# A fused attention and feed-forward kernel on one core: the first part of W_in moves to the head of GpSimd's DMA queue, the masks' distance tables move up, and later tiles are handled further ahead

## The chip, the cores and the metric

The kernel runs on one core of one Trainium2 chip. The metric is the time of one execution on the device in microseconds (us), taken as the median of seven executions. The profile is one further execution, recorded by the hardware profiler.

## The reference

Four batches with eight heads of 768 positions and head size 64 go through masked attention, and the result, seen as 3072 rows of 512, goes through two matrix products with an elementwise function between them:

```
scores = q @ k.T / 8  - slope[h] * dist          # dist = |i - j|, or 96 for the 8 global columns
keep   = (j < 8) or (0 <= i - j < 96)            # all else is masked out
x      = softmax(scores) @ v                     # 3072 x 512
h      = x @ w_in                                # 512 x 2048
out    = (h - tanh(h)) @ w_out                   # 2048 x 512
```

## The kernel before

The 3072 rows are cut into 24 tiles of 128 rows; tile u is block u // 4 of batch u % 4. A tile's attention needs only its own block of k and v (the "0" half) and, from tile 4 on, the block before it (the "1" half), into which the eight global columns are copied. The exponential's bias is not added but multiplied in afterwards, as a mask `mk` that is built once from three distance tables `rmat` ("dist" 0, 1 and 2).

The steps of one tile, with the names that the text uses and their lines:

- ("ld", "k"/"q"/"v", u), L578: a DMA from GpSimd's queue that also casts to bf16. For tile 0, k and q come instead by SyncE's queue as fp32 into `kf` (L569) and are cast by VectorE (L374). v of tile 0 and v of tile 1 come by GpSimd like the others.
- ("T", "k"/"q", u), L435: four TensorE transposes for tiles 0 to 7, with a copy out of PSUM ("Te", L372 or L374). From tile 8 on it is a DMA transpose from SyncE's queue.
- ("S", u, o), L384: scores. ("E", u, o, half), L389: exponential on ScalarE. ("M", u, o), L394: VectorE multiplies by the mask.
- ("AV", u), L403 and L405: the product with v. ("R"), L412, and ("N"), L420 or L422: the row sums' reciprocals and the scaling into `x`.
- ("Xt", u), L435, and ("X", u), L372 or L374: transposes x for tiles 0 to 5, and its copy into `xT`. From tile 6 on this too is a DMA transpose.

The rows then go through the two products in groups: tiles 0 to 3 each alone, from then on two tiles a group. ("m1", g, f), L448, is a part of the product with W_in, ("th"), L681, the tanh, ("g"), L457, the difference. The second product is "m2" (L489, L470) or, for groups 6 to 12, seven block products "P" (L316). For tiles 0 to 3, m1 with f = 0, 4, 8 and 12 needs the first, second, third and fourth part of W_in, called ("in", 0) to ("in", 3) and loaded on L546; ("out", j), L551, are the parts of W_out. The smaller `warm` matmuls on zeros (L666) fill the gaps that are foreseen on TensorE before ("S", 3, 0).

No engine chooses its order while it runs. A `Planner` simulates five engines and two DMA queues with given costs, and the sequence that it makes for each engine is what is emitted. So a change of its constants or of an op's conditions can move instructions on every engine, and the number of warm matmuls with them. Each engine, and each DMA queue, works strictly in its sequence. The list `arrive` gives the order of the transfers in GpSimd's queue: each waits for the issue of the one before. `ahead(u)` says how many tiles ahead of m1's progress tile u's attention may begin; from tile 6 on (`GATE`) its loads carry a semaphore wait for the m1 part from which they may start, half a tile (`EARLIER`) before its attention.

Of the kernel before, what the change touches and what calls it, by code (L numbers as in the profile page):

```python
# [13 lines left out]
PE, ACT, DVE, POOL, SP = ENG.PE, ENG.Activation, ENG.DVE, ENG.Pool, ENG.SP  # L14


class Planner:
# [20 lines left out]
    def run(self, free, prefer):  # L38
# [3 lines left out]
        held, freed = {}, {}  # L42
        uses, until = dict(self.uses), {}
        rings = {SP: [], POOL: []}
        setup, finish = {SP: 1.0, POOL: 1.8}, {SP: 0.35, POOL: 0.5}
        at_dma = 0.0
        mode = None
        done, start = {}, {}
# [3 lines left out]
        order = []  # L52
# [46 lines left out]
        while left:  # L99
# [5 lines left out]
            for key, n in cand:  # L105
# [4 lines left out]
                for eng, us in o["engs"]:  # L110
                    t = max(t0, free[eng])
# [16 lines left out]
            _, key, t, eng, us = best  # L128
# [38 lines left out]
def kernel(  # L167
# [47 lines left out]
    pl = Planner()  # L215
# [118 lines left out]
    def build_dist(m):  # L334
        def fill(r, base, value):
            nc.gpsimd.iota(
                r, pattern=[[1, P]], base=base, channel_multiplier=-1, allow_small_or_imprecise_dtypes=True,
            )
            if base == 0:
                nc.gpsimd.affine_select(  # L340
                    r, r, pattern=[[1, P]], base=0, channel_multiplier=-1, compare_op=ALU.is_ge, fill=value,
                )
            nc.gpsimd.affine_select(
                r, r, pattern=[[-1, P]], base=L - 1 - base, channel_multiplier=1, compare_op=ALU.is_ge, fill=value,
            )

        if m == 0:
            nc.vector.tensor_copy(out=rmat[0], in_=rmat[1])
            nc.vector.tensor_scalar_min(rmat[0][0:G, :], rmat[1][0:G, :], float(L))
        else:  # L350
            fill(rmat[m], P if m == 2 else 0, BIG)
        if m == 2:
            nc.gpsimd.memset(rmat[m][0:G, :], float(L))
# [154 lines left out]

    T_LD, T_V, T_W, T_ST, T_TR = 0.86, 1.13, 2.65, 0.4, 0.97
    AHEAD, EARLIER = 4.5, 0.5  # L510
    MORE = 0.0
    LATE = 2.0

    def ahead(u):
        return AHEAD + MORE * min(max(u - 8, 0) / 6.0, 1.0)

    arrive = [("t", 0), ("t", 1), ("t", 2), ("in", 0), ("t", 3), ("in", 1), ("in", 2), ("in", 3), ("t", 4), ("t", 5), ("out", 0), ("out", 1), ("out", 2), ("t", 6), ("out", 3), ("t", 7)]
    arrive += [("t", u) for u in range(NU) if ("t", u) not in arrive]
    GATE = 6

    prog = []
    gates = {}
    acc = 0.0
# [3 lines left out]
            prog.append((acc, ("m1", g, f)))  # L527
            acc += len(us) * per / CF

    pl.op(("dist", 1), POOL, 1.1, lambda e: build_dist(1), after=[("issue", ("ld", "k", 2))], pri=-2)  # L530
    pl.op(("dist", 0), DVE, 0.3, lambda e: build_dist(0), after=[("dist", 1)], pri=-2)
    pl.op(("dist", 2), POOL, 1.1, lambda e: build_dist(2), after=[("issue", ("in", 1))], pri=-1.5)
    for m in range(3):
        for half in range(2):
            pl.op(("mk", m, half), ACT, 0.85, lambda e, m=m, half=half: build_mask(m, half),
                  after=[("dist", m), ("mk", 0, 1) if m == 1 else None],
                  pri=-2 if m == 0 else 1)
    pl.op(("ident",), POOL, 0.6, lambda e: make_identity(nc, ident), after=[("issue", ("ld", "k", 1))], pri=-3)

    prev = None  # L540
    for it in arrive:
        kind, j = it
        if kind == "in":
            key = ("in", j)
            w = DFF // WJ
            pl.op(key, POOL, 0.8, lambda e, j=j, w=w: nc.gpsimd.dma_start(out=w_in_bf[j], in_=w_in_r[:, :, j * w : (j + 1) * w]),  # L546
                  after=[prev and ("issue", prev)], dma=T_W)
            prev = key
        elif kind == "out":
            key = ("out", j)  # L550
            pl.op(key, POOL, 0.8, lambda e, j=j: nc.gpsimd.dma_start(out=w_out_bf[j], in_=w_out_r[:, j * FJ : (j + 1) * FJ, :]),  # L551
                  after=[prev and ("issue", prev)], dma=T_W)
            prev = key
        else:
            u = j
            for nm, u in ([(nm, u) for nm in "kqv"] if u > 1 else [("k", 0), ("q", 0)] if u == 0 else
                          [("k", 1), ("q", 1), ("v", 0), ("v", 1)]):
                src = {"k": k, "q": q, "v": v}[nm]
                hw = u in hw_loads
                key = ("ld", nm, u)  # L560
                if nm == "v":
                    take = [(vname(u), ("vb", u))]
                    dst = lambda u=u: bufs[vname(u)][got["vb", u]][:, :, 0:Dh]
                else:
                    take = [(nm + "b", (nm + "b", u))]
                    dst = lambda u=u, nm=nm: buf(nm + "b", (nm + "b", u)).rearrange("p (h d) -> p h d", h=H)
                if hw and nm != "v":
                    pl.op(("ldf", nm, u), SP, 0.6,
                          lambda e, u=u, nm=nm, src=src: nc.sync.dma_start(out=buf("kf", ("kf", nm, u)), in_=rows(src, u)),  # L569
                          take=[("kf", ("kf", nm, u))], dma=T_LD)  # L570
                    pl.op(key, [(DVE, 0.43), (ACT, 0.6)], None,
                          lambda e, u=u, nm=nm, dst=dst: copy(e, dst(), buf("kf", ("kf", nm, u))),
                          after=[("ldf", nm, u)], take=take, give=[("kf", nm, u)])
                else:
                    go = [kk for a, kk in prog if a <= u - ahead(u) - EARLIER] if u >= GATE else []
                    if go:
                        gates[key] = go[-1]
                    pl.op(key, POOL, 0.88, lambda e, u=u, src=src, dst=dst: nc.gpsimd.dma_start(out=dst(), in_=rows(src, u)),  # L578
                          after=[prev and ("issue", prev), go[-1] if go else None], take=take, dma=T_V if nm == "v" else T_LD,
                          pri=-1 if u < GATE else 0)  # L580
                    prev = key

    for u in range(NU):
# [4 lines left out]
        for nm in ("k", "q"):  # L588
# [3 lines left out]
            if u < NPE:  # L592
                pl.op(("T", nm, u), PE, 0.24,
                      lambda e, u=u, nm=nm: pe_T(buf("bank", ("T", nm, u)), buf(nm + "b", (nm + "b", u))),
                      after=[("ld", nm, u), ("ident",), ("issue", last) if last else None], take=[("bank", ("T", nm, u))],
# [5 lines left out]
                      after=[("T", nm, u)], take=[(nT, tT)], give=[("T", nm, u)])  # L601
            else:
                pl.op(("T", nm, u), SP, 1.25,
                      lambda e, u=u, nm=nm, nT=nT, tT=tT: nc.sync.dma_start_transpose(
                          out=bufs[nT][got[tT]], in_=buf(nm + "b", (nm + "b", u))),
                      after=[("ld", nm, u), go], take=[(nT, tT)], give=[(nm + "b", u)], dma=T_TR, lag=LATE)
        Te = (lambda nm, u: ("Te", nm, u) if u < NPE else ("T", nm, u))
        os_ = (0, 1) if i else (0,)
        for o in os_:
# [3 lines left out]
                  after=[Te("q", u), go] + ([("issue", ("S", u, 0)), ("K", w) if i >= 2 else None] if o else [Te("k", u)]),  # L613
                  take=[("bank", ("S", u, o, hh)) for hh in range(2)] + [("po" if o else "pd", ("p", u, o))],
                  give=[("qT", u)] + (kgive if i >= 2 else []), mode="half", pri=0)
        for o in os_:
            for hh in range(2):
                pl.op(("E", u, o, hh), ACT, 0.53, lambda e, u=u, o=o, hh=hh: a_E(u, o, hh),
                      after=[("S", u, o), ("issue", ("E", u, 0, 1)) if o else None, ("issue", ("E", u, o, 0)) if hh else None],
                      give=[("S", u, o, hh)])  # L620
            pl.op(("M", u, o), DVE, 0.7, lambda e, u=u, o=o: a_M(u, o),
                  after=[("E", u, o, 0), ("E", u, o, 1)] + [("mk", 2 if o else min(i, 1), half) for half in range(2)])
        if 1 <= i < NQ - 1:
# [3 lines left out]
              after=[("M", u, 0), ("M", u, 1) if i else None, ("ld", "v", u), ("V", w) if i >= 2 else None, ("vone",)],  # L627
# [16 lines left out]
        if u < NPX:  # L644
            pl.op(("Xt", u), PE, 0.24,
                  lambda e, u=u: pe_T(buf("bank", ("X", u)), buf("x", ("x", u)).rearrange("q h d -> q (h d)")),
                  after=[("N", u, 0), ("N", u, 1), ("ident",)], take=[("bank", ("X", u))], give=[("x", u)], mode="full")
# [25 lines left out]
    for g, us in enumerate(groups):  # L673
# [65 lines left out]
        for t, u in enumerate(us):  # L739
            if u == NU - 1:  # L740
                for qq in range(4):
# [4 lines left out]
                          pri=2, mode="full")  # L746
# [32 lines left out]
    def prefer(s, at):  # L779
        return (1 if share2[at[1]] + 2.5 <= share1[at[0]] else 2) if s == 1 else (2 if share2[at[1]] + 2.5 <= share1[at[0]] else 1)  # L780

    order, done = pl.run({PE: 1.6, ACT: 2.1, DVE: 0.8, POOL: 0.7, SP: 0.7}, prefer)
    tc.plan = (order, done, pl)

    with tc.manual_schedule(engines={PE, ACT, DVE, POOL, SP}):
# [50 lines left out]
```

## Time and profile before

| | |
|---|---|
| median of 7 executions | 212.03 us (211.4 to 212.63) |
| the profiled execution | 211.4 us, its span from first to last instruction 209.6 us |
| granted TensorE clock | 0.999 |
| TensorE matmul, busy | 201.5 us, 96% of the span |
| VectorE, ScalarE, GpSimd, busy | 159.7, 143.2 and 70.1 us |
| DMA by GpSimd's queue (q0) | 13.37 MB in 77024 packets, 83.8% of the span on 16 engines |
| DMA by SyncE's queue (q1) | 13.38 MB in 32768 packets, 37.3% |

The profiled execution took as long as the shortest of the seven. Busy time of TensorE includes the 36 warm matmuls that the profile holds, which compute nothing. DMA shares of the queues overlap, so that together they may pass 100%.

### The profile page before, as it was taken

How to read it: one execution, taken by the hardware profiler on the slowest of the kernel's cores; microseconds unless marked ns; L12 is line 12 of the kernel's file. 1: busy time of each engine (PE TensorE's matmuls, PEld its weight loads, DVE VectorE, ACT ScalarE, POOL GpSimd, SP SyncE). 2: the span in 40 equal slices, each digit the busy share in tenths (PEclk: the TensorE clock that was granted, in tenths of full speed). 3: DMA queues.
4: the chain of work that ended last, by engine and by line, in shares of the span. 5: the costliest groups of instructions: out<-in, count | busy, mean ns of one | idle time of the engine just before them, and what ended most of it. 6: DMA issues, size and time to landing. Idle time of an engine off the chain costs nothing.

```text
span 209.6 us, 5798 instructions
## 1 busy us (share of the span) xinstructions
PE 201.5 (96%) x2281; PEld 161.6 (77%) x2292; DVE 159.7 (76%) x344; ACT 143.2 (68%) x349; POOL 70.1 (33%) x90
## 2 busy tenths in 40 slices
PE   5988999999999999999999999999999999999994
PEld 3757999565686766667888988988988989888853
DVE  2564798989276677759889999989999989898620
ACT  2399979678489788776776857887885784435311
POOL 7998375550055315045135225315225000000000
PEclk9999999999999999999999999999999999999999
DMA  9999999999979998999999997999999913002022
GB/s 130 122 145 190 198 166 207 182 166 185 166 122 141 133 175 125 106 153 104 174 103 86 215 128 123 153 134 138 140 118 160 127 28 117 9 3 100 0 103 100
DMA packets 109820, 27.12 MB, mean 129 GB/s; under 512 B 102497, under 2 KB 106849, under 8 KB 109793
## 3 DMA queue, kind: packets, MB, share of 16 engines
q0 software_dynamic: 77024, 13.37, 83.8%
q1 hardware_dynamic: 32768, 13.38, 37.3%
q8 instruction: 18, 0.29, 0.6%
q14 instruction: 10, 0.07, 0.1%
HBM read 27.26 MB, written 6.29 MB: 160 GB/s over the span
## 4 chain that ended last, share of the span: by engine, by line
PE 78%; issue 0%; ACT 0%
PE bank L448 34%; PE bank L316 21%; PE bank L489 12%; PE bank L384 5%; PE bank L405 2%; PE bank L403 2%; PE bank L470 2%; PE bank L435 0%; ACT ot L372 0%
## 5 line engine op out<-in xcount | busy, mean ns | idle before, releaser
L448 PE MATMUL bank<-xT,w_in_bf 128*128 128x256 bf16 (+1 forms) x896 | 97.2, 257 | 1.5 <-DMA w_in_bf<-in_moe_w_in_dram 1.4
L448 PEld LDWEIGHTS <-w_in_bf 128*128 128x128 bf16 x896 | 75.6, 98 | 12.6 <-DMA w_in_bf<-in_moe_w_in_dram 1.8
L681 ACT ACTIVATE th<-bank 128x512 f32<-128x512 f32 x96 | 56.7, 610 | 32.0 <-PE bank L448 23.4
L457 DVE TENSOR_TENSOR g<-bank,th 128x512 bf16<-128x512 f32 x80 | 53.3, 683 | 11.7 <-ACT th L681 11.6
L578 POOL DMA_DIRECT2D kb<-in_k_dram x23 | 20.6, 895 | 81.5 <-PE bank L448 57.2
L389 ACT ACTIVATE pd<-bank 128x512 bf16<-128x512 f32 x48 | 26.2, 602 | 10.2 <-PE bank L384 9.9
L316 PEld LDWEIGHTS <-hb 128*128 128x128 bf16 x280 | 27.1, 98 | 3.1
L420 ACT ACTIVATE x<-bank,rden 128x64 bf16<-128x64 f32 x104 | 23.1, 319 | 4.9 <-DVE rden L412 4.9
L290 DVE TENSOR_TENSOR hb<-g 128x1024 bf16<-128x1024 bf16 x35 | 22.9, 681 | 0.1
L578 POOL DMA_DIRECT2D vb<-in_v_dram x24 | 21.5, 897 | 3.4 <-DMA w_out_bf<-in_moe_w_out_dram 2.1
L389 ACT ACTIVATE po<-bank 128x512 bf16<-128x512 f32 x40 | 22.1, 616 | 0.0
L316 PE MATMUL bank<-bsum,hb 128*128 128x256 bf16 x168 | 21.6, 273 | 0.0
L578 POOL DMA_DIRECT2D qb<-in_q_dram x23 | 20.6, 894 | 1.4 <-DMA w_out_bf<-in_moe_w_out_dram 1.2
L394 DVE TENSOR_TENSOR pd<-pd,mk 128x1024 bf16<-128x1024 bf16 x24 | 16.5, 688 | 5.9 <-ACT pd L389 5.6
L489 PE MATMUL bank<-w_out_bf,g 128*128 128x512 bf16 x73 | 18.9, 379 | 0.4
L394 DVE TENSOR_TENSOR po<-po,mk 128x1024 bf16<-128x1024 bf16 x20 | 13.8, 689 | 2.1 <-ACT po L389 1.9
L489 PE MATMUL bank<-w_out_bf,hb 128*128 128x512 bf16 x60 | 14.8, 379 | 0.2
L384 PE MATMUL bank<-qT,kT 64*128 64x128 bf16 x352 | 14.6, 221 | 0.1
L384 PEld LDWEIGHTS <-kT 64*128 64x128 bf16 x352 | 10.3, 96 | 5.6 <-issue 5.0
L316 PE MATMUL bank<-bsum,g 128*128 128x256 bf16 x112 | 14.5, 273 | 0.0
L316 PE MATMUL bank<-w_out_bf,hb 128*128 128x256 bf16 x112 | 14.5, 273 | 0.0
L403 PE MATMUL bank<-vb,pd 128*128 128x65 bf16 x192 | 14.0, 193 | 0.0
(58 smaller groups left out, 197.1 us busy)
## 6 DMA issues: line engine op xcount, KB each, us to landing
out_dram<-ot SPq DMA_DIRECT2D x7, 512.0 KB, 3.9
vb<-in_v_dram POOLq DMA_DIRECT2D x24, 128.0 KB, 6.2
kb<-in_k_dram POOLq DMA_DIRECT2D x23, 128.0 KB, 4.4
qb<-in_q_dram POOLq DMA_DIRECT2D x23, 128.0 KB, 5.3
out_dram<-ot SPq DMA_DIRECT2D x9, 256.0 KB, 4.0
w_in_bf<-in_moe_w_in_dram POOLq DMA_DIRECT2D x4, 512.0 KB, 9.3
w_out_bf<-in_moe_w_out_dram POOLq DMA_DIRECT2D x4, 512.0 KB, 10.8
xT<-x SPq DMA_TRANSPOSE x18, 5.2
```

The costliest lines, as they stand in the source:

```text
L290: eng_of(e).tensor_tensor(out=out, in0=x, in1=y, op=ALU.add if sign > 0 else ALU.subtract)
L316: nc.tensor.matmul(o, a, b, start=(f == 0), stop=(f == CH - 1))
L384: nc.tensor.matmul(t[hh][:, p * P : (p + 1) * P], kt[r, p, :], qt[r, p, :], start=True, stop=True)
L389: nc.scalar.activation(dst, t, AF.Exp, bias=0.0, scale=scale)
L394: nc.vector.tensor_tensor(out=p, in0=p, in1=mk[:, m, :, :], op=ALU.mult)
L403: nc.tensor.matmul(o, pd[:, slot(h), :], vd[:, h, 0 : Dh + 1], start=True, stop=w is None)
L420: nc.scalar.activation(x[:, h, :], t[:, h, 0:Dh], AF.Copy, bias=0.0, scale=rd[:, h, :])
L448: nc.tensor.matmul(t[:, (f - f0) * n : (f - f0 + 1) * n], w_in_bf[j][:, c, fo : fo + P], xt[:, c, 0:n], start=(c == 0), stop=(c == CD - 1),)
L457: nc.vector.tensor_tensor(out=dst, in0=t.rearrange("q (b n) -> q b n", n=n), in1=th.rearrange("q (b n) -> q b n", n=n), op=ALU.subtract,)
L489: nc.tensor.matmul(o, gblk(g, f, f + 1, t * P, t * P + P)[:, 0, :], w_out_blk(f, 0, DM), start=(f == 0), stop=(f == CF - 1),)
L578: pl.op(key, POOL, 0.88, lambda e, u=u, src=src, dst=dst: nc.gpsimd.dma_start(out=dst(), in_=rows(src, u)), after=[prev and ("issue", prev ...
L681: pl.op(("th", g, f), ACT, 0.55, lambda e, g=g, f=f: nc.scalar.activation(buf("th", ("th", g, f)), buf("bank", ("h", g, f)), AF.Tanh, bias ...
```

## The change

The order of transfers in GpSimd's queue changes at its head: ("in", 0) comes before everything but tile 0's k and q (which are SyncE's), and ("in", 1) comes before tile 3's loads. The distance table 1, from which tables 0 and 1 are made, is built as soon as v of tile 1 has been issued, and no longer after k of tile 2. `ahead(u)` grows from 4.5 tiles at tile 8 to 5.5 tiles at tile 14 and beyond. The Planner's own constants (start of the queues, set-up and end of a DMA, 1.2 us more for a part of a weight) change as well; they cost nothing on the chip but shape the order.

```diff
-        setup, finish = {SP: 1.0, POOL: 1.8}, {SP: 0.35, POOL: 0.5}
+        setup, finish = {SP: 1.1, POOL: 2.0}, {SP: 0.3, POOL: 0.5}
...
-    MORE = 0.0
+    MORE = 1.0
     LATE = 2.0
+    W_LATE = 1.2
 
     def ahead(u):
         return AHEAD + MORE * min(max(u - 8, 0) / 6.0, 1.0)
 
-    arrive = [("t", 0), ("t", 1), ("t", 2), ("in", 0), ("t", 3), ("in", 1), ("in", 2), ("in", 3), ("t", 4), ("t", 5), ("out", 0), ...
+    arrive = [("t", 0), ("in", 0), ("t", 1), ("t", 2), ("in", 1), ("t", 3), ("in", 2), ("in", 3), ("t", 4), ("t", 5), ("out", 0), ...
...
+    DIST1 = ("ld", "v", 1)
...
-    pl.op(("dist", 1), POOL, 1.1, lambda e: build_dist(1), after=[("issue", ("ld", "k", 2))], pri=-2)
+    pl.op(("dist", 1), POOL, 1.1, lambda e: build_dist(1), after=[("issue", DIST1)], pri=-2)
...
-                  after=[prev and ("issue", prev)], dma=T_W)
+                  after=[prev and ("issue", prev)], dma=T_W, lag=W_LATE)
...
-    order, done = pl.run({PE: 1.6, ACT: 2.1, DVE: 0.8, POOL: 0.7, SP: 0.7}, prefer)
+    order, done = pl.run({PE: 1.6, ACT: 2.1, DVE: 0.8, POOL: 1.25, SP: 0.75}, prefer)
```

The sequences that come out of it differ from those before as follows (warm matmuls as "w").

- GpSimd, before: k1, identity, q1, v0, v1, k2, dist 1, q2, v2, in 0, k3, q3, v3, in 1, dist 2, in 2, in 3, k4. After: in 0, k1, identity, q1, v0, v1, dist 1, k2, q2, v2, in 1, dist 2, k3, q3, v3, in 2, in 3, k4.
- TensorE, before: 10 w, T k0, 3 w, T k1, T q0, T q1, S0, S1, 7 w, T k2, 6 w, T q2, AV0, 1 w, S2, 3 w, AV1, Xt0, 5 w, m1(0,0), Xt1, AV2, T k3, T q3, m1(1,0), Xt2, 1 w, S3, m1(2,0), m1(0,4), AV3, m1(1,4), m1(2,4), m1(0,8).
- TensorE, after: 11 w, T k0, 9 w, T q0, 2 w, S0, T k1, 2 w, T q1, 3 w, S1, 7 w, AV0, T k2, AV1, T q2, 2 w, Xt0, 4 w, S2, m1(0,0), Xt1, 5 w, AV2, T k3, m1(1,0), T q3, Xt2, m1(0,4), m1(2,0), S3, m1(1,4), m1(2,4), m1(0,8), AV3.
- VectorE after, from its sixth step: T k0's copy, cast of q0, T q0's copy, dist 0, copies of T k1 and T q1, M0, M1, both R and both N of tile 0, both R and one N of tile 1, X0, M2, X1. Before, dist 0 stood behind the copies of T q0 and T q1, tile 0's R came ahead of M1, and tile 0's N was ScalarE's.
- ScalarE after: both halves of mask 0, E0 twice, E1 twice, both halves of mask 1, copies of T k2 and T q2, N of tile 1's second half, E2 twice. Before: E0, both halves of mask 0, E0, E1 twice, half of mask 1, N of tile 0 twice, E2 twice, N of tile 1.
- SyncE after: T k9 and T q9 come ahead of the stores of tiles 1 and 2 and of X7; before, they came behind them.
- From tile 8 on, loads, transposes, S and AV of a tile stand up to one tile earlier among the m1 parts. The m1, m2 and P parts are the same in number and size.

More of the change, by code (lines that the diff above doesn't have):

```diff
@@ L510 @@
     AHEAD, EARLIER = 4.5, 0.5
-    MORE = 0.0
+    MORE = 1.0
     LATE = 2.0
+    W_LATE = 1.2
     def ahead(u):
         return AHEAD + MORE * min(max(u - 8, 0) / 6.0, 1.0)
-    arrive = [("t", 0), ("t", 1), ("t", 2), ("in", 0), ("t", 3), ("in", 1), ("in", 2), ("in", 3), ("t", 4), ("t", 5), ("out", 0), ("out", 1), ("out", 2), ("t", 6), ("out", 3), ("t", 7)]
+    arrive = [("t", 0), ("in", 0), ("t", 1), ("t", 2), ("in", 1), ("t", 3), ("in", 2), ("in", 3), ("t", 4), ("t", 5), ("out", 0), ("out", 1), ("out", 2), ("t", 6), ("out", 3), ("t", 7)]
     arrive += [("t", u) for u in range(NU) if ("t", u) not in arrive]
     GATE = 6
+    DIST1 = ("ld", "v", 1)
     prog = []
@@ L551 @@
             pl.op(key, POOL, 0.8, lambda e, j=j: nc.gpsimd.dma_start(out=w_out_bf[j], in_=w_out_r[:, j * FJ : (j + 1) * FJ, :]),
-                  after=[prev and ("issue", prev)], dma=T_W)
+                  after=[prev and ("issue", prev)], dma=T_W, lag=W_LATE)
             prev = key
```

## The prediction

> **What bounds the kernel.** I read the page's groups first, then TensorE's waits, then its busy time by stretch. In the first fence a row ends with the idle time ahead of the group and what ended it; the second is the whole list of TensorE's waits by the view of waits; the third gives stretch, its length, busy time (instructions), granted clock, DMA share and GB/s.
>
> ```profile
> L448 PE MATMUL bank<-xT,w_in_bf 128*128 128x256 bf16 (+1 forms) x896 | 97.2, 257 | 1.5 <-DMA w_in_bf<-in_moe_w_in_dram 1.4
> ```
>
> ```profile
> PE bank L435 <- DVE kb L374: 1.5, 1, 1.5
> PE bank L448 <- DMA w_in_bf<-in_moe_w_in_dram: 1.4, 2, 1.0
> PE bank L666 <- DVE zeros L668: 1.1, 1, 1.1
> PE bank L435 <- ACT x L420: 0.4, 2, 0.2
> ```
>
> ```profile
> 13.50:16.30 2.80, 1.43 (x15) 1.00 1.78 175
> 22.50:30.00 7.50, 7.50 (x142) 1.00 1.99 174
> 44.00:100.00 56.00, 55.58 (x580) 1.00 1.44 141
> 100.00:200.00 100.00, 99.95 (x1131) 1.00 1.03 108
> ```
>
> TensorE bounds the kernel from 22.5 us to the end: no wait is left and it is busy throughout. Its useful work is the same after the change, so the end moves by what the change takes from, or adds to, its idle and warm time before 22.5 us, unless it makes a new wait later. That early time is held by two arrivals of W_in, in the timeline (start, length, engine, line; in brackets the idle time before):
>
> ```profile
> 4.91 0.61 PE L435 MATMUL bank<-ident,kb 128*128 128x128 bf16 x4 [1.53 <-DVE kb L374]
> 5.90 0.71 DVE L374 CAST qb<-kf 128x512 bf16<-128x512 f32 x1
> 6.66 1.05 PE L435 MATMUL bank<-ident,qb 128*128 128x128 bf16 x8
> 7.30 0.87 DVE L374 COPY qT<-bank 128x512 bf16<-128x512 bf16 x2 [0.26 <-PE bank L435]
> 8.09 0.24 DVE L348 COPY rmat<-rmat 128x128 f32<-128x128 f32 x1
> 8.36 0.21 DVE L349 TENSOR_SCALAR rmat<-rmat 8x128 f32<-8x128 f32 x1
> 8.89 1.69 ACT L358 ACTIVATE mk<-rmat 128x128 bf16<-128x128 f32 x8
> 10.49 1.55 ACT L389 ACTIVATE pd<-bank 128x512 bf16<-128x512 f32 x3
> 16.33 1.07 PE L448 MATMUL bank<-xT,w_in_bf 128*128 128x128 bf16 x16 [1.03 <-DMA w_in_bf<-in_moe_w_in_dram]
> 21.42 1.07 PE L448 MATMUL bank<-xT,w_in_bf 128*128 128x128 bf16 x16 [0.32 <-DMA w_in_bf<-in_moe_w_in_dram]
> ```
>
> m1(0,0) starts at 16.33 with W_in's first part, m1(0,4) at 21.42 with its second. The copy of tile 0's xT ends at 14.78 + 0.42 = 15.20, so the first part is 1.1 us late.
>
> **W_in's first part first.** It removes both waits: issued at about 1.25 instead of 9.16, part 1 is in long before 15 us; part 2 is now ahead of tile 3's three loads (3 x 0.88 = 2.6 us of queue), so it lands by 21.4 - 2.6 = 18.8 us and is wanted at about 19.8, behind AV2 and m1(1,0). What is late next is tile 0's own chain, which I follow in the new sequences:
>
> - T k0 stays at 4.91. Its four loads of weights take 0.34, and nine warm matmuls stand between it and T q0. The first ten took 2.32 us from first start to last end, the last alone 0.42, so 0.21 apart: 9 x 0.21 = 1.9. T q0 starts at 7.15 (6.66 before).
> - T q0 to its copy 0.64 (6.66 to 7.30), the copy 0.42: 8.2. Dist 0 is now behind this copy and takes 0.48 (8.09 to 8.57): 8.7. GpSimd makes dist 1 by 7.4 in either order, as two moved issues balance, so it does not decide.
> - Mask 0 at 8.8, followed by the next step 1.60 later (8.89 to 10.49). E0 and E1 are four of 0.48 apart, the last 0.6: 8.8 + 1.6 + 3 x 0.48 + 0.6 = 12.4.
> - Two branches. VectorE: M1 0.68, R 0.30, both N 0.76, then R and N of tile 1 some 0.65, X0 0.42: 15.3. ScalarE: two halves of mask 1 in 1.6, the copies of T k2 and T q2 0.5 and 0.6: 15.1, then S2 with 0.34 on TensorE. m1(0,0) starts at about 15.5, 0.8 earlier than before.
> - Part of that is given back. AV2 needs M2: N of tile 1 0.9, two E 1.1, M 0.68, and three hand-overs of 0.1, from 15.1: 17.9. TensorE fills the time with Xt1 and five warm matmuls.
>
> From AV2 on I see no wait. Before m1(1,4), AV2, T k3, T q3, Xt2, S3, m1(1,0), m1(2,0) and m1(0,4) are issued; AV3, which stood ahead of it, now comes later. In issue time: 0.27 + 3 x 0.24 + 0.34 + 3 x 0.89 = 4.0, so m1(1,4) starts at 21.9; with the 0.27 of AV3 still owed, that compares as 22.2 with 22.57 before. The gain is 0.4 us. Bounds: 0.8 (all of m1(0,0)'s gain is kept) and, if k1 and q1 land so late that S1 holds E1, about zero.
>
> The last case needs a price: in 0 now stands ahead of every GpSimd load. During W_in alone the DMA moves at this rate:
>
> ```profile
> 20.00:22.00 2.00, 0.71 (x2) 1.00 1.24 206
> ```
>
> 0.524 MB at 206 GB/s are 2.5 us. k1, issued at 1.25, landed 4.4 later, at 5.65; it then lands at about 8.2, q1 at 9.0, v0 at 9.9, v1 at 10.8, q2 at 12.5. AV0 wants v0 at 12.1 and T q2 its load at 13. q1 must be in by 9.6 for S1 to reach E1 in time. That is hidden by 0.6 us, and this cover is thin: when it is gone, each us of q1's delay costs as much at the end.
>
> **The masks' distances.** Dist 1 goes ahead of k2's issue: k2 is 1.1 us later in GpSimd's sequence, which the transfer of in 0 hides, since the DMA is behind the issues by then. Cost nothing; without the cover, T k2 has another 0.8 us before the copy on ScalarE wants it.
>
> **Later tiles further ahead.** Loads and attention of tiles after 8 come up to a tile earlier. Loads wait in GpSimd's queue for an m1 part or a free buffer; GpSimd has 50 us and more of idle time and nobody waits for its next instruction. SyncE's queue now has T k9 and T q9 ahead of X7; X7 landed at 58.6 where m1 wanted it at 62.2, 3.6 us of cover against two issues of 1.3. TensorE has no wait after 22.5 us that could go, so the profiled execution gains nothing here; I take zero. Its bounds: -0.6 (the seven runs spread from 211.4 to 212.63 and the profiled one is at the lower end, so others may hold such a wait) and +0.6 (as much, made anew).
>
> **The sum.** The profiled execution took 211.4 us, 1.8 more than its span: 211.4 - 0.4 = 211.0. The median lies 0.63 above that execution; I keep the distance: 212.03 - 0.4 = 211.6.
>
> **Rivals.** (a) *Tile 0's q is held up by in 0.* The fp32 loads of tile 0 are on SyncE's queue, and now meet a weight part on the same engines instead of a small load:
>
> ```profile
> kf<-in_k_dram SPq DMA_DIRECT2D x1, 256.0 KB, 3.3
> kf<-in_q_dram SPq DMA_DIRECT2D x1, 256.0 KB, 4.0
> ```
>
> q0 landed at 1.27 + 4.0 = 5.3 and was cast at 5.90. k1, on the other queue, landed at 5.65, so that the two overlapped at their ends. If what is left of q0 must wait for all of in 0, it lands at 7.8, T q0 starts at 8.55 and not 7.15, and everything in the list above is 1.4 later: 1.4 - 0.4 = 1.0 slower, 213.0. It decides from the point where T q0 starts after 7.55 (no gain left), that is q0 after 6.8. For it speaks that dist 0 and so mask 0 now hang behind T q0's copy; against it, that q0 landed 1.2 us after tile 0's k although k1 was coming in: 0.262 MB in 1.2 us are 218 GB/s, no slower than W_in alone.
>
> The Trainium skill ("DMA: Bandwidth & Descriptors", Queues, rings and completion order) says that a DMA engine changes between queues only after a whole packet of some 9 to 17 descriptors. By that rule alone q0's rest would wait for large packets of the weight, once or twice, and the sum would go towards this rival's 213.0, and by the row of q0 beside k1 it stays at 211.6; no run here shows the two together.
>
> (b) *More is gained.* Part 2 of W_in, which TensorE waited for at 21.42, comes with 1 us or more to spare; executions longer than the profiled one may have waited longer for it. Then the whole spread above the fastest goes too: 212.03 - 0.4 - 0.6 = 211.0. For it: both early waits are for transfers. Against: no trace shows a longer run.
>
> (c) *A new wait in the steady part*, such as X behind T in SyncE's queue: 0.5 to 1 us, 212.3. Against it is the cover of 3.6 us above.
>
> **How the numbers follow.** Forecast 0.43, (a) 0.28, (b) 0.21, (c) 0.08. A measurement of this kernel tells about 0.3%, 0.64 us, from no change. The forecast, from 210.9 to 212.1 in its own bounds, is mostly inside that and a quarter of it faster; (b) is faster; of (a) three quarters are slower, of (c) half. Faster 0.33, same 0.41, slower 0.26. The range reaches from (b)'s 210.9 to just past (a), 213.1.
>
> **What would show it.** Right: T q0 at about 7.2, m1(0,0) at 15.5 and no wait for w_in_bf in TensorE's waits; nothing new after 23 us. Wrong: a cast of qb after 6.8 (rival a), an S1 that waits for q1's load, TensorE waits for kT or qT after 44 us (c), or more than 0.8 us gained (b).

## The result, and the profile after

The median of the kernel after is 213.71 us (27 executions) against 212.02 for the kernel before (64 executions beside it); the ratio is 1.0052 (95% interval 1.0034 to 1.007). The ratio leaves out executions more than 1.5% above the fastest of their kernel, seven of the 27 here, which the medians hold: the loss is 1.1 us by the ratio and 1.7 us by the medians. The forecast was 211.6 us, 0.4 us faster. The profiled execution took 213.74 us, its span is 211.9 us, 2.3 us more than before.

TensorE's waits (line, what it waited for, us in total, times, longest) have lost W_in, as forecast, and got others:

```profile
PE bank L435 <- DVE qb L374: 2.0, 1, 2.0
PE bank L435 <- DVE kb L374: 1.2, 1, 1.2
PE bank L668 <- DVE zeros L670: 1.1, 1, 1.1
PE bank L384 <- DMA qT<-qb: 0.9, 1, 0.9
PE bank L403 <- DVE pd L394: 0.8, 2, 0.4
```

The 1.4 us for `w_in_bf` are gone; 2.0 us for tile 0's cast q are new, and so are 0.9 us of a scores step for a transposed q. The stretches (length, TensorE's busy time, weight loads, VectorE, ScalarE, GpSimd, granted clock, DMA share, GB/s) show that the second lies late, where the kernel before had 99.95 of 100 us:

```profile
22.50:30.00 7.50, 7.50 (x142) 7.29 (x140) 5.54 (x13) 6.56 (x18) 4.48 (x6) 1.00 2.05 172
100.00:200.00 100.00, 99.11 (x1102) 86.95 (x1100) 88.77 (x175) 63.93 (x148) 20.14 (x23) 1.00 0.97 101
```

The timeline of the kernel after, at the lines shown of before:

```profile
8.54 0.65 DVE L374 CAST qb<-kf 128x512 bf16<-128x512 f32 x1 [2.71 <-DMA kf<-in_q_dram]
9.24 0.61 PE L435 MATMUL bank<-ident,qb 128*128 128x128 bf16 x4 [1.96 <-DVE qb L374]
11.73 0.63 PE L435 MATMUL bank<-ident,qb 128*128 128x128 bf16 x4
17.59 1.07 PE L448 MATMUL bank<-xT,w_in_bf 128*128 128x128 bf16 x16
21.61 1.95 PE L448 MATMUL bank<-xT,w_in_bf 128*128 128x128 bf16 x32
111.34 0.62 PE L384 MATMUL bank<-qT,kT 64*128 64x128 bf16 x16 [0.89 <-DMA qT<-qb]
```

T q0 runs at 9.24 (forecast 7.15), T q1 at 11.73, m1(0,0) at 17.59 (forecast 15.5, before 16.33); m1(0,4) does not wait for W_in any more, and S of tile 16 waits at 111.34. Two of the signs of being wrong that the prediction named are here: a cast of qb after 6.8 (8.54) and a wait for qT after 44 us. Three rows of the DMA issues (queue, KB, us from issue to landing) say what came late at the start:

```profile
w_in_bf<-in_moe_w_in_dram POOLq DMA_DIRECT2D x1, 512.0 KB, 8.2
kf<-in_q_dram SPq DMA_DIRECT2D x1, 256.0 KB, 7.2
kb<-in_k_dram POOLq DMA_DIRECT2D x1, 128.0 KB, 8.2
```

W_in's first part, issued at 1.25, took 8.2 us. Tile 0's q took 7.2 (4.0 before), and tile 1's k, issued at 2.14, landed at 10.29 (5.65 before, forecast 8.2); tile 1's q followed at 11.13 (forecast 9.0, wanted by 9.6).

A ledger helps with all that follows. m1(0,8), the product with W_in's third part, is the first step after which TensorE is full but for the waits named below, and the last block of m2 (the second half of L470) is one of the last. Both starts are from the trace (us); the sum is the start of the last block. Waits that the text gives to the hundredth are how far a step starts behind its place, 0.03 to 0.14 us more than the idle time in the views.

| kernel | m1(0,0) | m1(0,8) | from there to the last block | sum |
|---|---|---|---|---|
| before | 16.33 | 24.36 | 181.25 | 205.61 |
| after | 17.59 | 25.62 | 182.28 | 207.90 |
| e8, after once more | 17.73 | 25.56 | 182.19 | 207.75 |
| e1, k1 first | 15.51 | 24.08 | 182.82 | 206.90 |
| e9, half a part first | 15.43 | 24.04 | 182.30 | 206.34 |
| e7, k1 first and slack | 15.97 | 23.99 | 181.75 | 205.74 |
| e12, part first and slack | 16.43 | 24.46 | 181.74 | 206.20 |
| e10, k1 and q1 first, slack | 17.10 | 25.48 | 181.75 | 207.23 |
| e4, before with `MORE = 1.0` | 16.27 | 25.30 | 181.66 | 206.96 |
| e11, before with slack | 15.97 | 24.26 | 182.08 | 206.34 |

The loss of 2.29 us between these two executions is 1.26 before m1(0,8) and 1.03 after it. In the new sequence AV3 (0.25 us, from 22.32 to 22.57 in the kernel before) stands behind m1(0,8) and no longer ahead of it, so the loss is about 1.5 early and 0.75 late.

### The profile page after: what moved, and what is told of

Same layout as the page of the kernel before. It is cut to its first block, busy times and chain, and to the rows that moved or that the text cites. A ratio compares the mean times of both kernels' runs of the same rounds, so it can differ in the third digit from the quotient of the medians.

```text
span 211.9 us, 5815 instructions
## 1 busy us (share of the span) xinstructions
PE 201.9 (95%) x2291; PEld 162.4 (77%) x2301; DVE 160.9 (76%) x347; ACT 141.4 (67%) x340; POOL 70.1 (33%) x90
## 4 chain that ended last, share of the span: by engine, by line
PE 76%; DMA 11%; ACT 5%; issue 4%; DVE 1%; POOL 1%; SPq 0%; POOLq 0%; ACTq 0%
PE bank L448 34%; PE bank L316 18%; PE bank L489 12%; PE bank L384 5%; DMA kf<-in_q_dram 3%; DMA qb<-in_q_dram 3%; DMA qT<-qb 2%; PE bank L403 2%; DMA kT<-kb 2%; PE bank L405 2%; PE bank L435 2%; PE bank L470 2%; ACT mk L358 2%; ACT pd L389 1%; ACT x L420 1%
## 5 line engine op out<-in xcount | busy, mean ns | idle before, releaser
L457 DVE TENSOR_TENSOR g<-bank,th 128x512 bf16<-128x512 f32 x80 | 53.4, 683 | 10.3 <-ACT th L683 10.1
L420 ACT ACTIVATE x<-bank,rden 128x64 bf16<-128x64 f32 x96 | 21.2, 314 | 3.0 <-DVE rden L412 3.0
L384 PEld LDWEIGHTS <-kT 64*128 64x128 bf16 x352 | 10.3, 95 | 6.8 <-issue 5.5
## 6 DMA issues: line engine op xcount, KB each, us to landing
w_out_bf<-in_moe_w_out_dram POOLq DMA_DIRECT2D x4, 512.0 KB, 11.4
```

The lines of the kernel that those rows point to most:

```text
L384: nc.tensor.matmul(t[hh][:, p * P : (p + 1) * P], kt[r, p, :], qt[r, p, :], start=True, stop=True)
L420: nc.scalar.activation(x[:, h, :], t[:, h, 0:Dh], AF.Copy, bias=0.0, scale=rd[:, h, :])
L457: nc.vector.tensor_tensor(out=dst, in0=t.rearrange("q (b n) -> q b n", n=n), in1=th.rearrange("q (b n) -> q b n", n=n), op=ALU.subtract,)
```

## The experiments

Theory 1: in 0 holds up tile 0's q (rival (a)). Theory 2: it holds up tile 1's k and q behind it in GpSimd's queue, beyond the cover of 0.6 us. Theory 3: the new places of the later tiles make waits of their own.

**e1: tile 1's k first.** The order of two issues on GpSimd is exchanged; every other sequence is as in the kernel after.

```diff
+    swap = [("in", 0), ("ld", "k", 1)]
+    at = [next(i for i, o in enumerate(order) if o[2] == kk) for kk in swap]
+    a, b = order[at[0]], order[at[1]]
+    order[at[0]], order[at[1]] = (b[0], b[1], *a[2:]), (a[0], a[1], *b[2:])
```

> The changed kernel with every engine's sequence kept, except that GpSimd issues k of tile 1 first and W_in's first part second. Theory 1 (W_in's first part, coming first on the shared DMA engines, holds back the rest of tile 0's fp32 q, and mask 0, E0 and all behind hang on that q): with a small load between them q0 lands at 5.3 to 5.6 instead of 8.5, T q0 starts at 7.2, m1(0,0) at 15.6 instead of 17.6, m1(1,4) at 22.0 instead of 23.8; 1.7 us less, 212.0 us, ratio to before 1.000. Theory 2 (it is tile 1's loads behind W_in that come too late for S1): q1, v0 and v1 stay where they are, T q0 stays at 9.2, at most 0.3 us less, ratio 1.006. Theory 3 (the loss is made by the later tiles' new places): nothing moves, ratio 1.008.

Measured: 212.98 us, ratio 1.0028 (0.9995 to 1.0062). The timeline has T q0 at 7.08 and m1(0,0) at 15.51, which the prediction had as 7.15 and 15.5:

```profile
7.08 0.55 PE L435 MATMUL bank<-ident,qb 128*128 128x128 bf16 x4
10.17 0.40 PE L435 MATMUL bank<-ident,qb 128*128 128x128 bf16 x4 [1.07 <-DMA qb<-in_q_dram]
15.51 1.07 PE L448 MATMUL bank<-xT,w_in_bf 128*128 128x128 bf16 x16
```

So the prediction's chain through tile 0 holds here, though T q1 still waits for q1. The time of 212.0 us that theory 1 expected is missed: m1(0,8) comes 1.5 us earlier, but the end only 1.0, since S of tile 16 now waits 1.06 us and S of tile 18 0.34. It does not tell theory 1 from 2, as q0 too landed in time.

**e2, e3, e4: the parts of the change alone.** e2 is the kernel after with `MORE = 0.0` (no growth of the lead), e3 the kernel before with the new `arrive` and the earlier dist 1 and all its own constants, e4 the kernel before with `MORE = 1.0`.

> The changed kernel with later tiles as far ahead as before (MORE = 0.0). Theory 1: the first 45 us are unchanged, q0 lands late at about 8.5 and m1(0,0) starts at about 17.6; only the wait of 1.0 us ahead of S of tile 16 may go: 212.7 to 213.7 us, ratio 1.003 to 1.008. Theory 3 (the later tiles' places are the whole loss): 212.0, ratio 1.000.

> The kernel before with GpSimd's new order alone (W_in's first part first, its second ahead of tile 3, distance 1 behind the second v); the planner's constants and the later tiles as before. Theory 1: q0 lands at about 8.5 here too, but in this sequence distance 0 and mask 0 stand ahead of q0's cast, so less hangs on it: T q0 at about 9.3, m1(0,0) at 16.5 to 16.8, total 212.3 to 213.5 us, ratio 1.001 to 1.007. Theory 3: as the kernel before, 1.000. Were q0 not late, T q0 would still wait for T k1 ahead of it, at about 9.0, so its landing and not T q0 tells.

> The kernel before with later tiles up to one tile further ahead alone (MORE = 1.0). Theory 1: the early part is as before (m1(0,0) at 16.3), no new wait that matters, 212.0 within 0.4 us, ratio 0.998 to 1.002. Theory 3: most of the loss shows here, 213 to 213.7 us, ratio 1.005 to 1.008.

| | time, us | ratio | what TensorE waits for |
|---|---|---|---|
| e2 | 217.36 | 1.0218 (1.0158 to 1.0278) | 2.3 us for qT at tile 20 |
| e3 | 213.76 | 1.0066 (1.0035 to 1.0097) | 2.1 us for k1, 0.6 us for qT at tile 22 |
| e4 | 213.48 | 1.0053 (1.0019 to 1.0087) | m1(0,4) 1.3 us for W_in's second part |

No part gains by itself. e2 missed both expectations (212.7 to 213.7, and 212.0): from m1(0,8) on its profiled execution took 186.05 us, and with the wait of 2.3 us at tile 20 came a granted clock of 0.50 from 150.7 to 154.1 us; the rest of its loss was not followed up. e3 shows the head's loss without any replanned lead: q0 landed 3.8 us after its issue, in time, and k1 8.1 after its own:

```profile
PE bank L435 <- DMA kb<-in_k_dram: 2.1, 1, 2.1
```

e4 has no wait for a transposed q, and e2, with a shorter lead, has the largest, so it is not the longer lead alone that makes these waits; the change's other constants move the loads and transposes as well. Still e4 has the time that theory 3 expected (213.0 to 213.7) and theory 1 did not (212.0 within 0.4). In its profiled execution 0.94 us are lost up to m1(0,8) and 0.41 from there on, without a wait. The first is at a place where the kernel before waits as well: W_in's second part let m1(0,4) start at 22.37 in this execution and at 21.42 in that of before. All DMA issues up to W_in's last part, at 15.0 us, stand within 0.03 us of those of before, and no transfer of SyncE's queue runs between 5.3 and 47.9 us, so nothing in this trace leads from the longer lead to that landing. Why the twelve executions of e4 are slower remains open.

**e8: the kernel after, unaltered, on another chip.**

> The changed kernel again, unaltered, for a second profile and on one chip with the next three. Theory 1 in the form that the first runs leave (q0's rest meets W_in's first part on single DMA engines, so the delay differs from run to run: q0 landed 7.2, 6.3 and 3.8 us after its issue in three kernels with this head of the queue): q0 lands anywhere from 5 to 9 us, 213.5 us, ratio to before 1.005, and the runs spread wider than those of before. Were the delay a fixed cost of the order, it would be 8.5 again within 0.3.

Measured: 212.9 us, ratio 1.0034 (1.0013 to 1.0055). This execution separates theories 1 and 2 by itself, because q0 happened to land in time:

```profile
7.09 0.63 PE L435 MATMUL bank<-ident,qb 128*128 128x128 bf16 x4
10.52 0.61 PE L435 MATMUL bank<-ident,kb 128*128 128x128 bf16 x4 [1.66 <-DMA kb<-in_k_dram]
```

T q0 is at 7.09, yet T k1 waits 1.66 us for a k1 that landed at 10.47, and m1(0,0) starts at 17.73, no earlier than the 17.59 with q0 late. Theory 1 falls as the cause: the loss is as large with q0 in time. In the profiled execution of the kernel after, q0's delay comes on top of k1's by at most the 0.6 us that T k1 (10.90) started behind k1's landing (10.29).

**e5: e1 with the later loads released half a tile earlier.**

```diff
-                        gates[key] = go[-1]
+                        gates[key] = [kk for a, kk in prog if a <= u - ahead(u) - EARLIER - 0.5][-1]
```

> e1 (k of tile 1 ahead of W_in's first part, all sequences of the changed kernel otherwise) with the later tiles' loads allowed half a tile (some 3.7 us) earlier by their semaphore waits; sequences kept. Theory 4 (what is left of the loss is S waiting for the transposed q, since the load of q, its transpose and the neighbours' transfers come close to each other in the new places): loads land earlier, the waits for qT (1.3 us in e1, at tiles 16 and 18) go, 1.0 to 1.4 us less than e1: 211.6 to 212.0, ratio 0.998 to 1.000. Rival (the DMA engines as such are the limit there, earlier loads only take from the transposes before them): as e1, ratio 1.003, with waits at other tiles.

Measured: 213.08 us, ratio 1.004 (1.0011 to 1.0069). The waits moved to S of tiles 17 (0.38 us), 18 (0.55) and 21 (0.52), and T q4 waited 0.87. The rival's numbers came: earlier loads alone do not heal the late term. That the DMA engines are the limit there, which is the rival's reason, was not shown.

**e6 and e7: e1 replanned with slack.** The Planner allows 1 us more for each DMA transpose, a longer lead from the start and loads a whole tile ahead; `MORE` is 0.5 in e6, 0 in e7.

```diff
-    AHEAD, EARLIER = 4.5, 0.5
-    LATE = 2.0
+    AHEAD, EARLIER = 5.0, 1.0
+    LATE = 3.0
```

> e1 with the later tiles planned anew: a DMA transpose reckoned 1 us longer (LATE = 3.0), loads a whole tile ahead of the attention (EARLIER = 1.0), attention 5.0 to 5.5 tiles ahead (AHEAD = 5.0, MORE = 0.5). Theory 4: no wait for qT, the early gain of 0.1 to 0.4 us is kept: 211.6 to 212.0, ratio 0.998 to 1.000, and runs spread less. Rival: the loss is in the more frequent changes between score and full matmuls (38 after 44 us, 36 in e1): no better than e1, 1.003.

> As e6 with MORE = 0.0 (attention 5.0 tiles ahead throughout). Theory 4: as e6 or 0.2 us more (40 changes of matmul kind after 44 us): 211.8 to 212.2, ratio 0.999 to 1.001; so that slack and not MORE decides. Rival (being further ahead is what costs): better than e6 by 0.5 us or more.

Measured: 211.86 us, ratio 1.0006 (0.9983 to 1.0028), and 211.99, ratio 0.9996 (0.9977 to 1.0016). No wait for a transposed q is left in either; it lands 2.7 us or more ahead of its scores (e1: 0.14 us and less at tiles 11, 16 and 18). With both causes removed the kernel is as fast as before, and not faster.

**e9: half of W_in's first part first.** The kernel after, with the part cut into two DMAs: the first half stands where the part stood, the second (`w_in_rest`) behind tile 1's q.

```diff
+            nc.gpsimd.dma_start(out=w_in_bf[0][:, :, 0 : w // 2], in_=w_in_r[:, :, 0 : w // 2])
...
+    q1 = pl.ops[("ld", "q", 1)]["fn"]
+    pl.ops[("ld", "q", 1)]["fn"] = lambda e: (q1(e), w_in_rest())
```

> The kernel after with all sequences kept, but W_in's first part goes in two halves: its first half at the head of GpSimd's queue, its second half (of the same 0.26 MB) behind tile 1's q. Theory (tile 1's k and q wait for the bytes ahead of them): k1 landed at 6.2 with nothing ahead of it and at 10.3 to 10.5 with the whole part ahead, so with half of it at about 8.3, q1 at 9.1, T q1 at 9.2 to 9.5, and m1(0,0) at 15.5 to 15.9 instead of 17.6; the late wait of the 16th tile's scores stays, ratio to before 1.002 to 1.004. Rival (the first weight transfer is late by itself, whatever its size): k1 at 9.5 or later, m1(0,0) at 17 or later, ratio 1.005.

Measured: 212.2 us, ratio 1.0014 (0.9991 to 1.0038). k1 landed at 7.66, q1 at 8.71, T q1 ran at 9.16, m1(0,0) at 15.43, a little better than expected. So it is bytes ahead of k1 that cost, not that a weight comes first: k1 lands at 5.93 to 6.83 with no weight ahead (e1, e5, e6, e7, e14, e16), at 7.66 with 0.26 MB, at 9.70 to 10.47 with 0.52 MB (after, e2, e3, e8, e12, and e13 and e15 below). The late term is still there (182.30 us after m1(0,8)), but at another place: S of tile 16 got its q 0.26 us ahead, and T q4 waited for its load, 0.94 us behind its place. Less these waits, the kernel after (0.93), e1 (1.06 and 0.34) and e9 all take 181.35 to 181.42 us after m1(0,8). With the 0.25 of AV3 the kernel before would have 181.5, so these waits are as large as the late term.

**e10: k1 and q1 both ahead of W_in's first part, with e7's slack.**

> The replanned kernel with more slack (a transpose given 1 us more, loads a whole tile ahead, no growth of the lead), sequences kept, with tile 1's k, the identity and tile 1's q all ahead of W_in's first part. It had 211.99 us with T q1 at 10.63 and m1(0,0) at 15.97. Theory (m1(0,0) hangs on tile 1's q as long as q lands after 9.6, then on the masks): q1 lands at about 7, T q1 runs at 8.5 to 9.2, m1(0,0) at 15.1 to 15.5, no late wait; 211.3 us, ratio 0.995 to 0.998. Rival (the masks' chain on VectorE and ScalarE already sets m1(0,0)): m1(0,0) within 0.2 of 15.97 and 212.0, ratio 1.000. The price to watch is the first part of W_in, wanted at 15.1: it should land at about 10.

Measured: 213.19 us, ratio 1.0053 (1.0027 to 1.0079); both expectations failed. T q1 ran at 8.98, as hoped, but what stands behind the part is now v0, and AV0 waited for it:

```profile
PE bank L435 <- DMA kb<-in_k_dram: 1.3, 1, 1.3
PE bank L403 <- DMA vb<-in_v_dram: 1.2, 1, 1.2
```

The first row is T k2. After these two waits TensorE's clock was halved, as the stretches show (columns as above):

```profile
14.00:15.50 1.50, 1.24 (x21) 1.10 (x22) 0.64 (x3) 0.75 (x2) 1.50 (x3) 1.00 1.43 201
16.00:19.00 3.00, 3.00 (x29) 2.39 (x28) 0.92 (x2) 2.55 (x11) 2.15 (x3) 0.50 2.15 171
19.50:21.00 1.50, 1.50 (x31) 1.48 (x30) 1.26 (x6) 1.41 (x4) 1.01 (x2) 1.00 1.35 200
```

m1(0,8) starts at 25.48; from there it takes e7's 181.75 us to the hundredth. Nine of the twelve executions had a mean granted clock of 0.992 or less; the other three took 211.57, 211.85 and 213.8 us.

**e11: the kernel before with the slack alone.**

> The kernel before with the slack alone: a transpose given 1 us more, a lead of 5 tiles, loads a whole tile ahead; head of GpSimd's queue as before. Theory (the slack only heals waits that the new places made; the kernel before has none): m1(0,0) at 16.3, m1(0,4) at about 21.4, no late wait, 212.0 us, ratio 0.998 to 1.002. Rival (the slack is worth something of its own, and the two kernels with it hide a loss that the queue's head makes): 211.0 or less, ratio under 0.997.

Measured: 212.89 us, ratio 1.0051 (1.0022 to 1.008). Neither: the slack costs. TensorE waits nowhere late, but from m1(0,8) on it takes 182.08 us against 181.25. In the new sequence it changes 42 times between scores and other matmuls after 45 us, against 36 before and in the kernel after; e7 has 40. A step of 16 score matmuls takes 0.55 us from its first matmul to the next product, and two steps of 8 take 0.66, so that scores cost more when they stand apart. How much more is easily read wrongly: the traces of the kernel after, e7 and e11 lack 10 or 11 of the 144 m2 matmuls, and a score step seems 0.23 us longer where the record behind it is missing. So the same program has 12.16 us of scores from m1(0,8) on in e7 and 11.48 in e16, whose records are complete, and the kernel after 11.72 in its first profile and 11.27 in e13; the kernel before has 11.27, with no step lengthened. The slack thus costs some 0.2 us of scores in e7 and e16, and in e11 (12.30, less two lengthened steps 11.85) up to 0.6 of its 0.8; the rest of e11's loss is open. The 12.2 us against 11.3 in the expectation of e16 below do not compare like with like.

**e12: the slack with W_in's part first.**

> The kernel after with the slack (a transpose given 1 us more, loads a whole tile ahead, no growth of the lead), W_in's first part at the head of GpSimd's queue as in the change. Against the same kernel with tile 1's k first (211.99) only the first two transfers differ. Theory (the queue's head costs at the end what it costs at m1(0,0) as soon as no late wait is left): k1 lands at 10.3, m1(0,0) at 17.4 to 17.9, no late wait; 1.3 to 1.9 slower, 213.3 to 213.9 us, ratio 1.006 to 1.009. Rival (the early loss is made up later, and the late waits alone make the change slower): 212.0 to 212.6, ratio under 1.003.

Measured: 212.54 us, ratio 1.0025 (1.0004 to 1.0046): the rival's numbers, but not its reason. k1 landed at 9.70, earlier than in the two profiles of the kernel after, and m1(0,0) started at 16.43, 0.46 later than in e7. The end is 0.46 later too (206.20 and 205.74): the early term is smaller here than expected, but it goes to the end undiminished where no late wait is met.

These 0.46 us are not q1's landing, which is 10.54 here and 10.58 in e7. They arise behind it (T q1 and S1, first of e7, then of e12):

```profile
10.63 0.40 PE L435 MATMUL bank<-ident,qb 128*128 128x128 bf16 x4 [0.82 <-DMA qb<-in_q_dram]
11.54 0.40 PE L384 MATMUL bank<-qT,kT 64*128 64x128 bf16 x8 [0.19 <-DVE qT L374]
10.58 0.62 PE L435 MATMUL bank<-ident,qb 128*128 128x128 bf16 x4
11.78 0.61 PE L384 MATMUL bank<-qT,kT 64*128 64x128 bf16 x8
```

The same matmuls take half as long again in e12. In every trace TensorE begins at half of its later pace: warm matmuls start 0.213 us apart, later 0.109. The full pace comes at 7.4 us in e1, 10.0 in e7, 11.1 in the kernel before, 13.2 in e12, 13.9 in the kernel after and 16.5 in e8. The views print a clock of 1.00 for this time, since the trace's record of the granted clock begins only with the full pace. With k1 first, five of six executions run at the full pace from 10.0 us on (e14 falls back from 11.8 to 15.2); all seven with the part first run at half pace between 12.2 and 13.1, three of them because they fell back (e3, e13, e15). So the part ahead of k1 costs in two ways: q1, which is behind both in either order, lands somewhat later (median 10.86 against 10.55), and tile 1's transposes and scores run more slowly. With the part first TensorE stands idle before T k1 (0.9 us in e12, 1.66 in e8); that this idling is what keeps the pace low was not tested.

**e13 to e16: two by two on one chip.** The kernel after had 213.71 us in the first measurement and 212.9 on another chip (e8), a difference as large as the terms, so the four combinations were run side by side: W_in's part or k1 first, the change's sequences or those with slack. e13 is the kernel after, e14 as e1, e15 as e12, e16 as e7.

> The unaltered kernel after, beside the next three on one chip, as a table of two by two: W_in's first part or tile 1's k at the head of GpSimd's queue, with the sequences of the change or those with slack. Theory (two terms that add: the head's loss early, 0.5 to 1.5 us at the third quarter of W_in, m1(0,8), and the later tiles' places 0.5 to 1 us from there to the end): 213.3 to 213.8 us, ratio 1.005 to 1.008, m1(0,8) at 25.5 and 182.2 us from there to the last matmul of m2. Rival A (the later places make all of it): the same here. Rival B (the head makes all of it): the same here.

> The kernel after with tile 1's k ahead of W_in's first part, sequences kept: the early term is taken away, the late one stays. Two terms: 0.5 to 1.2 us less than the unaltered kernel after, 212.4 to 212.9 us, ratio 1.002 to 1.004; m1(0,8) at 24.1, 182.3 to 182.8 from there. Rival A (the later places make all of it): as the unaltered kernel after within 0.3 us. Rival B (the head makes all of it): as the kernel before, ratio within 0.0015 of 1.

> The slack's sequences with W_in's first part at the head as in the change: the late wait is taken away, the early term stays. Two terms: 0.4 to 1.0 us less than the unaltered kernel after, 212.4 to 213.0, ratio 1.002 to 1.005; m1(0,8) at 24.5 to 25.5 and 181.75 from there. Rival A: as the kernel before, ratio within 0.0015 of 1. Rival B: as the unaltered kernel after.

> Both taken away: the slack's sequences and tile 1's k first. Two terms: 211.9 to 212.1, ratio 0.999 to 1.001; m1(0,8) at 24.0 and 181.75 from there. That nothing is gained is put down to score matmuls standing apart: 40 changes between scores and other matmuls after 44 us in TensorE's sequence against 36 in the kernel before, and 12.2 us for the scores after m1(0,8) against 11.3.

| | the change's sequences | with slack |
|---|---|---|
| W_in's part first | 213.58, ratio 1.0079 (1.0048 to 1.011) | 212.69, 1.0014 (0.9985 to 1.0042) |
| k1 first | 212.71, 1.0035 (1.0018 to 1.0053) | 211.68, 1.0002 (0.9981 to 1.0022) |

By the medians, exchanging the first two transfers takes away 0.87 us, the slack 0.89, both 1.90; by the ratios it is 0.9, 1.4 and 1.6 us. The executions of one cell spread over 1.3 to 2.2 us, and e13 has only six, so that the two terms add is shown to no better than about 1 us. Rival A (the later places make all of it) fails at e14, 0.87 us below e13 where it asked for 0.3 at most, though e15's ratio is as near to 1 as it asked. Rival B (the head makes all of it) fails at e14's ratio and at e15's time. The late term is plain in the traces: from m1(0,8) on e13 took 182.38 us and e14 181.87, e15 and e16 181.75 each. The early term is not: m1(0,8) is at 24.44, 25.27, 24.59 and 24.08 in e13 to e16, where 25.5 was expected of e13 and 24.1 of e14. In e14's profiled execution W_in's part landed only at 10.29 and T q1 waited 2.0 us for q1, although k1 came first; in e13's it landed at 8.94. The clock was 0.50 for 3.4 us from about 12 us on in both, and in e15's.

## Why the prediction was wrong, point by point

- **TensorE is the bound from 22.5 us, and only idle and warm time can move the end**: right for the late part, where the waits account for the late term of the kernel after, e1 and e9 within 0.15 us. For the early part the prediction left out TensorE's pace, which made 0.5 us between e7 and e12.
- **W_in's waits go**: right; neither part of it is waited for.
- **Tile 0's chain gives m1(0,0) at 15.5**: right as a chain (15.51 in e1, 15.43 in e9), but it had the case where nothing ahead of it is late.
- **"From AV2 on I see no wait", and the gain of 0.4**: wrong. Where m1(0,0) did start at 15.5, TensorE waited for tile 3's loads, which the change puts behind W_in's second part: T q3 in e1 and T k3 in e9.

```profile
19.61 0.40 PE L435 MATMUL bank<-ident,qb 128*128 128x128 bf16 x4 [0.37 <-DMA qb<-in_q_dram]
18.45 0.40 PE L435 MATMUL bank<-ident,kb 128*128 128x128 bf16 x4 [0.40 <-DMA kb<-in_k_dram]
```

  In e1, e7, e9 and e16 m1(0,8) is at 23.99 to 24.08; with AV3's 0.25 that is 24.24 to 24.33, against 24.36 before. So at most 0.1 us is gained even without a late k1. (The prediction's terms for AV2 also come to 18.1, not 17.9.)
- **The size of in 0: the step that failed.** The prediction took 0.524 MB at 206 GB/s, 2.5 us, put k1 at 8.2 and q1 at 9.0 and called that hidden by 0.6 us. k1 landed at 9.70 to 10.47 in the seven executions with the part first, 4.1 to 4.8 us later than the 5.65 of before, and q1 at 10.54 to 11.36. In place of a gain of 0.4 us stood an early loss of 1.5 in the ledger; TensorE's slower pace (0.5, e12) and, in this one execution, tile 0's late q (at most 0.6) are parts of it. The trace shows two reasons for k1's landing. The 206 GB/s were those of 20 to 22 us; between 4.5 and 5.5 us the kernel after moved 82 GB/s, between 5.5 and 6.5 us 148:

```profile
4.50:5.50 1.00, 1.00 (x2) 1.00 0.92 82
5.50:6.50 1.00, 0.99 (x2) 1.00 0.99 148
```

  (length, GpSimd's busy time, clock, DMA share, GB/s.) And a load is in when its last DMA engine is through: by the trace's semaphore updates the first of the 16 engines had finished k1 at 8.17 and the last at 10.29, where before it was 5.07 and 5.64. So the first engine came 3.1 us later and the last 4.65: of the 2.1 us that the price of 2.5 us missed, some 0.6 are a slower rate of all engines and 1.5 the wider spread between them (an estimate from these four times). The Trainium skill ("DMA: Bandwidth & Descriptors", Why a DMA increments its semaphore by 16 and not by 1) says that the engines of a DMA finish independently and the semaphore counts them; this case agrees, and shows 2.1 us between the first and the last of them, 1.5 to 2.2 in the seven executions with the part first, against 0.6 in the kernel before and 0.3 in e11 (5.17 to 5.50), both without a weight next to k1.
- **"Each us of q1's delay costs as much"**: right in the slope. With q1 at 10.54, 10.66 and 10.86 (e12, e13, e15) m1(0,0) was at 16.43, 16.54 and 16.74, 5.9 us later each; with k1 first it was 5.4 us behind q1 (e1, e5, e6, e7, e16), so that a q1 at 10.12 still gave 15.51 in e1. That "q1 must be in by 9.6" fits the three with the part first, but the 0.5 us between 5.9 and 5.4 is TensorE's pace and not q1. In the two executions with the latest q1, 11.13 and 11.36 (after, e8), m1(0,0) came another 0.5 us later: in the first T k1 stood behind the late T q0, in the second the full pace came only at 16.5. The conversion was good; the q1 that went into it was 1.5 to 2.4 us off. The thin cover was named, its failure was put at "about zero" gain, and it was not made a rival of its own with a price and a chance.
- **Rival (a), tile 0's q held up by in 0**: happens, but does not decide (e8). In the profiled execution 15 engines had q0 by 5.61 and one at 8.51; in e8, e12, e13 and e15, with the same head, q0 landed 3.7 to 5.1 us after its issue, in e2 6.3 (4.0 before). So the rule of packets that the prediction quoted does not show as a fixed cost here. T k1 ran 0.6 us after k1's landing in the profiled execution, behind the late T q0, and that is about what this delay can have added there. Of the times of the forecast and its rivals, this one's 213.0 us is the nearest, by a mechanism that does not decide; that is luck.
- **Later tiles: zero, with bounds of 0.6**: wrong, by 0.75 us in the ledger and 0.89 in the medians. The cover that was priced, X in SyncE's queue, held; the one that broke was not looked at: from a tile's load through its DMA transpose to its scores. Before, tile 16's q was loaded from 104.78 to 109.19, transposed by 113.41 and wanted at 114.50. After, the chain of waits has

```profile
99.81 6.23 DMA qb<-in_q_dram
106.05 5.15 DMA qT<-qb
```

  issue 5.0 us earlier, but 11.4 us on the way instead of 8.6, while its scores stand 4.1 us earlier (110.4 without the wait). So 1.1 us of slack became a wait of 0.9. Rival (c) had the right size and the wrong place, and a wait for qT among its signs.
- **The chance** of slower, 0.26, and the top of the range, 213.1, were too low: a cover of 0.6 us was taken to hold, a slack of 1.1 us (tile 16's q) was not looked at, and the two failures together were in no rival.

## What to carry to other kernels

Moving a large transfer to the head of a queue moves its time onto everything behind it: where k1 was spared, the wait was for q1 (e1), then for v0 and k2 (e10), or for tile 3's k (e9). Work out a landing by the slowest DMA engine at that time of the run, not by a mean rate from elsewhere, and treat a cover smaller than that spread as gone. When a planner's constants change, measure the slack from landing to use for every tile, for a loss of 1 us may sit 90 us away from the edit, and a plan without waits can still lose: e11 lost 0.8 us that way, in part by scattering the scores. Before reading a difference of some tenths between two traces, look at two traces of the same program.

## What the runs showed of the hardware

- The landing of the first W_in part varies from one execution to the next: 8.8 to 9.6 us in the seven with the part first, 9.2 to 10.3 in six (e1, e5, e6, e7, e14, e16) with k1 first. Why single engines lag is open.
- TensorE starts at half of its later pace (256 columns in 0.213 us, later 0.109), and reaches the full one at 7.4 to 16.5 us, by kernel and execution (e12).
- TensorE's granted clock falls to 0.50 for some 3.4 us in part of the executions. Of 128 executions of the kernel before that ran beside the experiments, 26 had a mean clock of 0.992 or less, with a median of 213.1 us against 211.9 for the rest. The Trainium skill ("TensorE: Matmul & The Clock Gate", Part 1: The HAM clock gate) explains such halving by a free-running window of about 3.4 us, and advises to have no idle gaps above that. Length and depth agree; the gap does not: in e10 the longest wait ahead of it was 1.3 us, with AV0 between it and one of 1.2 us. How much idle time suffices was not tried.
